# One attention and MLP decode step: the vectors of w2 and wo in blocks of 128 columns, and one spreading of o

## The chip, the cores and the metric

The kernel runs on one core of a Trainium2 chip. Times are device microseconds (us) of one execution. The time before is the median of three runs, 99.37 us (99.36 to 99.45).

A core has five engines with instruction streams of their own: TensorE (PE in the profile, its weight loads PEld) multiplies into PSUM, VectorE (DVE) and ScalarE (ACT) compute elementwise, GpSimd (POOL) fills constants here and counts landings, and SyncE (SP) issues the transfers. Sixteen DMA engines move the data. Engines wait for one another through semaphores.

## The reference

One token x of 1,024 values is normalised to xn. Two branches read xn, and their results are added to x:

```python
x = A_x
xn = _layernorm(x, axis=-1)
return x + _A_ref(xn, A_k_cache, A_v_cache, A_wq, A_wo) + _B_ref(xn, B_w1, B_b1, B_w2, B_b2)
# _A_ref: q = xn @ wq (32 heads of 128); keys and values are the last 4096 of 65536 rows, 4 groups of 8 heads
#         o = softmax(q k^T / sqrt(128)) v ;  o as 4096 values @ wo (4096 x 1024)
# _B_ref: h = gelu(layernorm(xn) @ w1 + b1)  (3584 values);  h @ w2 (3584 x 1024) + b2
```

All inputs are bf16. Almost everything that is moved is weights and cache: wq 8 MB, w1 7, w2 7, wo 8, keys 4 and values 4.

## The kernel before

**Loads.** SP issues, in this order: wq's first half, keys 0, wq's second half, keys 1, w1 (lines 234 to 238); when the keys have been transposed on DVE, the values into the keys' place; when q is done, w2 in parts of 16 and 12 rows into wq's place; and when TensorE's w1 loop is done, wo in parts of 8, 12, 9, 2 and 1 rows (lines 310 to 321). A row is what one matmul contracts over: 128 partitions with 1,024 columns. wo's first 20 rows go to the tile BIG behind w2's 28, the last 12 (TAIL is 20) into the tile KT.

**TensorE in order.** It multiplies xn with wq, then q with the keys, then adds a bias row through EDGE, then multiplies with w1 in a loop of seven (lines 472 to 476), sums the softmax, transposes h, and multiplies the probabilities with the values (lines 488 to 491). Then come twelve rounds (label `pe_round`) that go over 48 rows, four to a round: seven rounds for w2, five for wo's first twenty rows. The twelve rows that are left are an unrolled tail (lines 529 to 540) with four small matmuls to a row. All rounds and the tail add into one PSUM bank.

**Vectors.** In a round the stationary operand is a window of 128 columns of the tile GO, which is zero but for the values wanted. A value stands at two columns 64 apart, so that a window lays it on two output rows; values follow one another two columns apart. GO holds three such vectors, G0 (12 values of h), G1 (16) and OT (32 values of o), of the sizes that PHASES = [3, 4, 5] gives in rounds, and from phase to phase the window jumps by SHIFT more. `twice` is the view that writes both copies. DVE writes G0 and G1 (line 370).

**The o turn.** The attention result ON (32 rows, DVE, line 386) has to become columns. Four matmuls do it at `pe_turn_o` (line 507) into PSUM bank 2, and DVE copies the 32 columns from there, twice each, into OT (line 389). `pe_turn_o` is one block in the loop and is entered at each phase's end but the last, so it is run twice: the first time its result is what DVE copies, the second time it is computed again and the wait asks for DVE's copy instead of ON (register `ready`).

**Counting.** A round waits for the semaphore s_feed to reach the register `turn`. GpSimd counts it up in program order (lines 401 to 414): one for each wq half and for each two transposed key parts, then, as parts of w2 and wo land, their number of rounds, and one for wo's nine rows. `pe_phase` waits for the next count too, so the tail begins when wo's nine rows are counted. GpSimd's constants (lines 177 to 225) stand ahead of that; the memset of GO is their last but one.

Of the kernel before, what the change touches and what calls it, by code (L numbers as in the profile page):

```python
# [5 lines left out]
ALU = mybir.AluOpType  # L6
ACTF = mybir.ActivationFunctionType
AX = mybir.AxisListType

D = 1024  # L10
# [7 lines left out]
FC = F // 128  # L18
# [3 lines left out]
WQ_CHUNKS = [4, 4]  # L22
# [4 lines left out]
PAIRS = 2  # L27
FAR = -1e30
XP = 72
TAIL = 20  # L30
TAIL_AT = [0, 512, 256, 768]
ROW = 31
LEAD = 32
COPY = 64
ROUND = 4
PHASES = [3, 4, 5]
SHIFT = 160


class Track:  # L40
# [11 lines left out]
def bass_parallel_sum__sliding_block_cached__mixer_channel_mlp__decode_kernel(  # L52
# [17 lines left out]
    pe, dve, act, pool, sp = nc.tensor, nc.vector, nc.scalar, nc.gpsimd, nc.sync  # L70

    def sems(name, n):
        return [nc.alloc_semaphore(f"{name}{i}") for i in range(n)]
# [5 lines left out]
    s_wo = sems("s_wo", len(WO_CHUNKS))  # L79
    s_w2 = sems("s_w2", len(W2_CHUNKS))  # L80

    DVE = Track(nc, "S_DVE")
    ACT = Track(nc, "S_ACT")
    POOL = Track(nc, "S_POOL")
    done = {n: nc.alloc_semaphore(f"S_PE_{n}") for n in (
        "x", "h", "hT", "q", "sc", "pv", "tot", "o2", "fin")}
    s_feed = nc.alloc_semaphore("S_FEED")

    def sb(name, shape, d):
        return nc.alloc_sbuf_tensor(name, shape, d)  # L90

    f32, bf16 = dt.float32, dt.bfloat16
# [23 lines left out]
    HT = sb("HT", [128, FC], f32)  # L116
    U2 = sb("U2", [128, FC], f32)
# [9 lines left out]
    SUMP = sb("SUMP", [128, 1], f32)  # L127
    REC = sb("REC", [64, 1], f32)
    ON = sb("ON", [32, DH], bf16)
    starts = [sum(2 * ROUND * n + SHIFT for n in PHASES[:k]) for k in range(3)]  # L130
    GO = sb("GO", [128, starts[2] + 192], bf16)
    G0, G1, OT = (GO[:, first:first + 192 - 8 * (k == 0)] for k, first in enumerate(starts))
    ONM = QBD[0:32, :].bitcast(f32)
    KV = sb("KV", [128, 16384], bf16)
    KT = sb("KT", [128, 16384], bf16)
# [4 lines left out]
    PS = nc.alloc_psum_tensor("PS", [128, 8 * 512], f32)  # L140
# [14 lines left out]
    C = {}  # L155
# [18 lines left out]
    def pool_wait():  # L174
        pool.wait_ge(POOL.sem, POOL.cnt)
# [6 lines left out]
        out=identb[:, :], in_=identb[:, :], pattern=[[-1, 128]], compare_op=ALU.not_equal,  # L182
# [16 lines left out]
        out=identf[:, :], in_=identf[:, :], pattern=[[-1, 128]], compare_op=ALU.not_equal,  # L199
# [15 lines left out]
    POOL.mark(pool.affine_select(  # L215
        out=HALF4[:, :], in_=HALF4[:, :], pattern=[[-16, 4]], compare_op=ALU.is_ge, fill=0.0,
# [26 lines left out]
    def layernorm_stats(src, n, name):  # L243
# [21 lines left out]
        out=XM.rearrange("p (a r) -> p a r", r=KC), in0=XN[:, :].rearrange("p (a r) -> p a r", r=KC),  # L265
        in1=identb[:, :].unsqueeze(2).to_broadcast([128, 128, KC]), op=ALU.mult))
    dve_wait()
    DVE.mark(dve.tensor_reduce(
        out=XNT[:, :], in_=XM.rearrange("p (a r) -> p r a", r=KC), axis=AX.X, op=ALU.add))
# [9 lines left out]
        out=B64[:, :].rearrange("p (k r) -> p k r", k=2),  # L279
        in_=identf[:, :].rearrange("p (q r) -> p r q", q=4).unsqueeze(1).to_broadcast([128, 2, 32, 4]),  # L280
# [36 lines left out]
    c0 = 0  # L317
    for j, n in enumerate(WO_CHUNKS):
        home, first = wo_home(c0)
        sp.dma_start(home[:, first:first + n * D], wo_flat[:, c0 * D:(c0 + n) * D]).then_inc(s_wo[j], 16)  # L320
        c0 += n

    def twice(vec, n):
        return vec[:, LEAD:LEAD + 2 * COPY].rearrange("p (u x) -> p u x", u=2)[:, :, 0:2 * n:2]

    S = PS[:, 3 * 512:7 * 512]
    for n in range(2):
        dve.wait_ge(done["sc"], 14 + 2 * n)
        C["mx"] = DVE.mark(dve.tensor_reduce(  # L329
            out=MX2[:, n:n + 1], in_=S[:, 1024 * n:1024 * n + 1024], axis=AX.X, op=ALU.max))  # L330
# [6 lines left out]
    for b in range(4):  # L337
        C["nmb"] = DVE.mark(dve.tensor_scalar(  # L338
            out=NMB[32 * b:32 * b + 32, :], in0=MXR[:, :], scalar1=-SCALE, scalar2=None, op0=ALU.mult))
    act.wait_ge(DVE.sem, C["nmb"])  # L340
    C["exp"] = ACT.mark(act.activation(  # L341
        out=Pb[:, :], in_=S, func=ACTF.Exp, bias=NMB[:, 0:1], scale=SCALE, accum_out=SUMP[:, 0:1]))
# [9 lines left out]
        out=HT[:, :].rearrange("p (t c) -> p c t", c=4),  # L352
        in0=PS[:, 2 * 512 + 32:2 * 512 + 64].rearrange("p (c t) -> p c t", c=4)[:, :, 0:7],
        in1=B1T[:, :].rearrange("p (t c) -> p c t", c=4), op=ALU.add))
# [11 lines left out]
    dve_wait()  # L366
    DVE.mark(dve.reciprocal(out=U2[:, :], in_=U2[:, :]))
    dve_wait()
    for vec, c0, n in ((G0, 0, PHASES[0] * ROUND), (G1, PHASES[0] * ROUND, PHASES[1] * ROUND)):
        C["d_GT"] = DVE.mark(dve.tensor_tensor(  # L370
            out=twice(vec, n), in0=HT[:, c0:c0 + n].unsqueeze(1).to_broadcast([128, 2, n]),
            in1=U2[:, c0:c0 + n].unsqueeze(1).to_broadcast([128, 2, n]), op=ALU.mult))

    dve.wait_ge(done["tot"], 1)
    DVE.mark(dve.reciprocal(out=REC[:, :], in_=PS[0:64, 2 * 512 + 64:2 * 512 + 65]))
# [2 lines left out]
    for i in range(2):  # L378
        rows = slice(32 * i, 32 * i + 32)
        DVE.mark(dve.scalar_tensor_tensor(  # L380
            out=ONM.rearrange("p (i c d) -> p i c d", i=2, c=PAIRS)[:, i],
            in0=PS[rows, 512:1024].rearrange("p (c i d) -> p i c d", c=PAIRS, i=2)[:, i], scalar=REC[rows, 0:1],
            in1=HALF[rows, :].unsqueeze(2).to_broadcast([32, PAIRS, DH]), op0=ALU.mult, op1=ALU.mult))
    dve_wait()
    with nc.allow_low_precision(reason="one of the four terms is not zero"):
        C["on"] = DVE.mark(dve.tensor_reduce(
            out=ON[:, :], in_=ONM.rearrange("p (g d) -> p d g", g=4), axis=AX.X, op=ALU.add))
    dve.wait_ge(done["o2"], 1)
    C["OT"] = DVE.mark(dve.tensor_copy(
        twice(OT, 32), PS[:, 2 * 512:2 * 512 + 32].unsqueeze(1).to_broadcast([128, 2, 32])))  # L390

    for engine, track, a in ((act, ACT, 1), (dve, DVE, 0)):
        engine.wait_ge(done["fin"], 1)
# [13 lines left out]
    pool.wait_ge(DVE.sem, C["kt", 3])  # L407
    pool.sem_inc(s_feed, 1)
    for semaphores, chunks in ((s_w2, W2_CHUNKS), (s_wo, WO_CHUNKS[:WO_HEAD])):
        for semaphore, n in zip(semaphores, chunks):  # L410
            pool.wait_ge(semaphore, 16)
            pool.sem_inc(s_feed, n // ROUND)
# [15 lines left out]
    turn = pe.alloc_register("turn")  # L428
# [40 lines left out]
    def h_cols(row, t):  # L469
        return row.rearrange("p (m a c) -> p m a c", m=128, a=7)[:, :, bass.ds(t, 1), :]  # L470

    pe.wait_ge(s_w1[0], 16)
    with pe.Fori(0, 7) as t:
        for k in range(KC):
# [15 lines left out]
            last = add(bank(1), PT[:, bass.ds(i * 256 + u * 64, 128)], V3[:, :, bass.ds(i * 1024 + u * 256, 256)])  # L490
        last.then_inc(done["pv"], 1)

    first_turn = 1 + len(WQ_CHUNKS) + PAIRS
    vec, column, limit, more, ready = (pe.alloc_register(n) for n in ("vec", "column", "limit", "more", "ready"))
    for register, value in ((vec, 0), (column, 0), (limit, first_turn + PHASES[0]), (more, PHASES[1]), (ready, C["on"])):
        pe.reg_mov(register, value)
    pe.wait_ge(DVE.sem, C["d_GT"])
    PEO = [pe.engine]
    at = type(pe.snap(turn)).of_register_unchecked
    vec_at, column_at = at(vec, min_val=0, max_val=starts[2] + 2 * ROUND * (PHASES[2] - 1)), at(  # L500
        column, min_val=0, max_val=(sum(PHASES) - 1) * ROUND * D)
    nc.br("pe_round", engines=PEO)
    with nc.body("pe_turn_o", valid_engines=PEO):
        pe.wait_ge(DVE.sem, ready)
        pe.reg_add(ready, ready, C["OT"] - C["on"])
        for j in range(4):
            last = pe.matmul(PS[:, 2 * 512:2 * 512 + 32], lhsT=E4[:, j * 128:(j + 1) * 128],
                             rhs=ON[:, j * 32:(j + 1) * 32], start=(j == 0), stop=(j == 3))
        last.then_inc(done["o2"], 1)
        pe.reg_add(vec, vec, SHIFT)  # L510
        pe.reg_add(limit, limit, more)
        pe.reg_add(more, more, PHASES[2] - PHASES[1])
        nc.br("pe_round", engines=PEO)
    with nc.body("pe_round", valid_engines=PEO):
        pe.wait_ge(s_feed, turn)
        pe.reg_add(turn, turn, 1)
        for u in range(ROUND):
            for a in range(2):
                add(bank(7), GO[:, bass.ds(vec_at + (LEAD + 2 * u - ROW - a), 128)],
                    BIG[:, bass.ds(column_at + (u * D + a * 512), 512)])  # L520
        pe.reg_add(vec, vec, 2 * ROUND)
        pe.reg_add(column, column, ROUND * D)
        pe.br_lt(turn, limit, on_true="pe_round", on_false="pe_phase")
    with nc.body("pe_phase", valid_engines=PEO):
        pe.wait_ge(s_feed, turn)
        pe.br_lt(turn, first_turn + sum(PHASES), on_true="pe_turn_o", on_false="pe_tail")
    nc.switch_bb("pe_tail")

    c0 = TAIL
    for j, n in enumerate(WO_CHUNKS[WO_HEAD:]):  # L530
        pe.wait_ge(s_wo[WO_HEAD + j], 16)
        for c in range(c0, c0 + n):
            home, column = wo_home(c)
            rhs = home[:, column:column + D]
            for a in range(4):
                first, column = LEAD + 2 * c - (0 if a % 2 else ROW), 7 * 512 + a // 2 * 256
                last = add(PS[32 * a:32 * a + 32, column:column + 256], OT[:, first:first + 32],
                           rhs[:, TAIL_AT[a]:TAIL_AT[a] + 256], tile_position=(0, 32 * a))
        c0 += n
# [31 lines left out]
```

## Time and profile before

| what | us |
|---|---|
| median of three runs | 99.37 |
| the profiled execution | 99.39 |
| its span | 98.0 |
| TensorE busy | 73.8 |
| VectorE busy | 38.2 |
| transfers, share of 16 engines, SP's queue | 95.5% |
| w1 loop ends, SP issues wo from | 62.6 |
| rounds begin | 73.13 |
| the tail's first load | 94.33 |
| last landing of wo | 95.89 |
| store issued | 96.79 |

The profile is of one execution. Its lines give, for groups of instructions, the engine, the kernel's line, the operation, and out<-in by the program's names. In the timeline a line starts with start and duration in us, xN is the number of instructions, and brackets hold the engine's idle time ahead of the group and what ended it. In the list of transfers the last number is the us from issue to landing. Because a helper records most matmuls, they all carry line 426 and are told apart by their operands: BIG with XZ is wq, BIG with YZ is w1, BIG with GO the rounds, KT with GO the tail. A few matmul records are missing from the trace.

### The profile page before, as it was taken

What the parts mean: (1) busy time and instruction counts of PE and PEld (TensorE: products, weight loads), DVE (VectorE), ACT (ScalarE), POOL (GpSimd) and SP (SyncE); (2) the same over time, 40 slices, a digit from 0 to 9 for tenths busy, and PEclk for the clock granted to TensorE, in tenths of its full rate; (3) what the DMA queues carried; (4) which work ended last, traced back from release to release, by engine and by line L of the source; (5) the groups of instructions that cost most, each with busy time, mean ns of one, the idle gap of its engine ahead of it and who ended that gap; (6) DMA issues with size and microseconds to landing.
All of it is one profiled execution on the core that took longest, in us unless ns stands there. A gap on an engine that the chain in (4) does not pass through costs nothing.

```text
span 98.0 us, 1273 instructions
## 1 busy us (share of the span) xinstructions
PE 73.8 (75%) x341; PEld 30.9 (32%) x353; DVE 38.2 (39%) x52; ACT 7.8 (8%) x14; POOL 9.3 (9%) x29
## 2 busy tenths in 40 slices
PE   0005000399999974999999999799969999999991
PEld 0001000033444421334434444333334444444450
DVE  0002899899920799950193620060034000000001
ACT  0500000600000023000005200200000000000001
POOL 6999200000000000000000000000000000000000
PEclk9999999999999998557999999999999999999999
DMA  6699999999999988889899999998999999999980
GB/s 201 254 442 429 402 430 442 428 455 428 408 435 528 609 375 375 375 375 468 375 428 428 435 515 455 428 428 375 411 391 428 428 482 421 401 421 451 395 324 1
DMA packets 2229, 39.88 MB, mean 407 GB/s; under 512 B 434, under 2 KB 436, under 8 KB 692
## 3 DMA queue, kind: packets, MB, share of 16 engines
q1 hardware_dynamic: 2020, 39.85, 95.5%
q10 hardware_dynamic: 208, 0.01, 0.1%
q8 instruction: 1, 0.02, 0.1%
HBM read 39.86 MB, written 0.00 MB: 407 GB/s over the span
## 4 chain that ended last, share of the span: by engine, by line
DMA 63%; PE 23%; DVE 8%; SPq 3%; issue 2%
DMA KT<-in_A_wo_dram 32%; DMA KV<-in_A_k_cache_dram 30%; PE PS L426 22%; DVE KT L285 4%; SPq L320 2%; DVE MX L329 1%; SPq L159 1%; DVE QBD L305 1%; DVE Pb L293 1%; SPq L232 1%; DVE Pb L395 0%; PE PS L464 0%
## 5 line engine op out<-in xcount | busy, mean ns | idle before, releaser
L426 PE MATMUL PS<-BIG,GO 128*128 x84 | 20.1, 379 | 1.5 <-DVE QBD L380 0.7
L285 DVE STREAM_TRANSPOSE KT<-KV 128x4096 bf16<-128x4096 bf16 x4 | 17.7, 4432 | 4.9 <-DMA KV<-in_A_k_cache_dram 4.9
L426 PE MATMUL PS<-BIG,XZ 128*128 x64 | 16.5, 426 | 0.0
L426 PEld LDWEIGHTS PS<-BIG,GO 128*128 x96 | 9.2, 98 | 11.6 <-issue 1.2
L426 PE MATMUL PS<-BIG,YZ 128*128 x56 | 12.4, 380 | 0.0
L426 PE MATMUL PS<-KT,QBD 128*128 x32 | 9.9, 486 | 1.6 <-DVE QBD L305 1.6
L426 PEld LDWEIGHTS PS<-BIG,XZ 128*128 x64 | 6.8, 107 | 10.1 <-issue 4.2
L426 PE MATMUL PS<-KV,KT 128*128 x32 | 8.3, 381 | 0.6
L423 PE MATMUL PS<-XBRP,HOT 1*128 1x512 bf16 x3 | 1.7, 618 | 9.0 <-DVE XZ L275 9.0
L426 PEld LDWEIGHTS PS<-BIG,YZ 128*128 x56 | 5.4, 96 | 6.8 <-issue 0.9
L395 DVE CAST Pb<-PS 64x256 bf16<-64x256 f32 x1 | 0.4, 417 | 17.6 <-PE PS L426 17.6
L419 PE MATMUL PS<-XBRP,onesb 1*128 1x512 bf16 x2 | 1.0, 602 | 8.2 <-DMA XBRP<-in_A_x_dram 8.2
L426 PEld LDWEIGHTS PS<-KT,QBD 128*128 x32 | 3.8, 119 | 7.7 <-issue 5.7
L245 DVE BATCH_NORM_STATS2 BN<-PS 128x6 f32<-128x512 f32 x2 | 1.3, 690 | 9.3 <-PE PS L419 9.3
L426 PEld LDWEIGHTS PS<-KV,KT 128*128 x32 | 3.1, 96 | 5.4 <-issue 4.0
L329 DVE TENSOR_REDUCE MX<-PS 128x1 f32<-128x1024 f32 x2 | 2.4, 1220 | 5.5 <-PE PS L426 5.5
L380 DVE SCALAR_TENSOR_TENSOR QBD<-PS,REC,HALF 32x256 f32<-32x256 f32 x2 | 0.9, 474 | 6.9 <-PE PS L426 6.9
L423 PEld LDWEIGHTS PS<-XBRP,HOT 1*128 1x128 bf16 x3 | 0.3, 118 | 10.2 <-DVE XZ L275 9.9
L345 DVE STREAM_TRANSPOSE KT<-Pb 128x2048 bf16<-128x2048 bf16 x1 | 2.3, 2311 | 2.1 <-ACT Pb L341 2.1
L341 ACT ACTIVATE Pb<-PS,NMB 128x2048 bf16<-128x2048 f32 x1 | 2.0, 1967 | 14.1 <-DVE NMB L338 14.1
L395 ACT ACTIVATE Pb<-PS 64x256 bf16<-64x256 f32 x1 | 0.4, 381 | 31.6 <-PE PS L426 31.6
L351 DVE TENSOR_TENSOR HT<-PS,B1T 128x28 f32<-128x28 f32 x1 | 0.2, 206 | 6.6 <-PE PS L482 6.6
(75 smaller groups left out, 36.6 us busy)
## 6 DMA issues: line engine op xcount, KB each, us to landing
BIG<-in_A_wq_dram SPq DMA_DIRECT2D x2, 4096.0 KB, 18.9
BIG<-in_B_w_dram SPq DMA_DIRECT2D x1, 7168.0 KB, 46.2
KV<-in_A_k_cache_dram SPq DMA_DIRECT2D x2, 2048.0 KB, 23.3
KV<-in_A_v_cache_dram SPq DMA_DIRECT2D x2, 2048.0 KB, 13.5
BIG<-in_B_w_dram SPq DMA_DIRECT2D x1, 4096.0 KB, 24.7
BIG<-in_B_w_dram SPq DMA_DIRECT2D x1, 3072.0 KB, 31.4
BIG<-in_A_wo_dram SPq DMA_DIRECT2D x1, 3072.0 KB, 25.5
KT<-in_A_wo_dram SPq DMA_DIRECT2D x1, 2304.0 KB, 30.6
```

The costliest lines, as they stand in the source:

```text
L159: sp.dma_start(dst[:, c0 * width:(c0 + n) * width].rearrange("p (c n) -> p c n", c=n), src[:, c0:c0 + n, :],).then_inc(semaphores[j], 16)
L232: sp.dma_start(KV[:, c * 8192:(c + 1) * 8192], pairs(A_k_cache, c)).then_inc(s_k[c], 16)
L245: DVE.mark(dve.bn_stats(out=BN[:, 12 * n + 6 * i:12 * n + 6 * i + 6], in_=src[:, 512 * i:512 * i + 512]))
L285: C["kt", n] = DVE.mark(dve.transpose(KT[:, n * 4096:(n + 1) * 4096], KV[:, n * 4096:(n + 1) * 4096]))
L293: C["qtb"] = DVE.mark(dve.transpose(QTB, Q32))
L320: sp.dma_start(home[:, first:first + n * D], wo_flat[:, c0 * D:(c0 + n) * D]).then_inc(s_wo[j], 16)
L329: C["mx"] = DVE.mark(dve.tensor_reduce(out=MX2[:, n:n + 1], in_=S[:, 1024 * n:1024 * n + 1024], axis=AX.X, op=ALU.max))
L341: C["exp"] = ACT.mark(act.activation(out=Pb[:, :], in_=S, func=ACTF.Exp, bias=NMB[:, 0:1], scale=SCALE, accum_out=SUMP[:, 0:1]))
L345: C["d_pt"] = DVE.mark(dve.transpose(PT[:, 0:2048], Pb[:, :]))
L419: last = pe.matmul(bank(i), lhsT=onesb[0:1, :], rhs=XB[0:1, 8 * i:8 * i + 8, :])
L423: pe.matmul(bank(n), lhsT=HOT[:, 8:136], rhs=XB[0:1, 0:8, :], start=True, stop=False, skip_group_check=True)
L426: return pe.matmul(to, lhsT=lhsT, rhs=rhs, start=False, stop=False, skip_group_check=True, **place)
```

## The change

GO is laid out by rounds. It now holds twelve blocks of 128 columns (STEP), one for each round, w2's seven first and then wo's five, and behind them OT with the twelve values of o for the tail only. In a block the four values stand two columns apart and once more 64 columns on. The window moves by STEP from round to round, without jumps.

DVE writes all seven blocks of w2 in one instruction. The o turn is run once, after four rounds (TURN), and then the limit of the loop is set to all twelve. ScalarE, not DVE, copies from PSUM: first the 20 columns that the rounds use, into the five blocks, then the 12 of the tail, without a second copy. TensorE's rounds no longer wait for that copy themselves; GpSimd waits for it ahead of its first count for wo. Three of the five register moves of the loop go ahead of w1's loop, and two are gone.

```diff
-PHASES = [3, 4, 5]
-SHIFT = 160
+ROUNDS = 12
+TURN = 4
+STEP = 128
...
-    GO = sb("GO", [128, starts[2] + 192], bf16)
-    G0, G1, OT = (GO[:, first:first + 192 - 8 * (k == 0)] for k, first in enumerate(starts))
+    GO = sb("GO", [128, ROUNDS * STEP + LEAD + 96], bf16)
+    OT = GO[:, ROUNDS * STEP + LEAD:]
...
-    def twice(vec, n):
-        return vec[:, LEAD:LEAD + 2 * COPY].rearrange("p (u x) -> p u x", u=2)[:, :, 0:2 * n:2]
+    def spread(first, n):
+        return GO[:, LEAD + first * STEP:LEAD + (first + n) * STEP].rearrange(
+            "p (r c y) -> p r c y", c=2, y=COPY)[:, :, :, 0:2 * ROUND:2]
+
+    def rows_of(values):
+        n = values.shape[1] // ROUND
+        return values.rearrange("p (r u) -> p r u", u=ROUND).unsqueeze(2).to_broadcast([128, n, 2, ROUND])
...
-    for vec, c0, n in ((G0, 0, PHASES[0] * ROUND), (G1, PHASES[0] * ROUND, PHASES[1] * ROUND)):
-        C["d_GT"] = DVE.mark(dve.tensor_tensor(
-            out=twice(vec, n), in0=HT[:, c0:c0 + n].unsqueeze(1).to_broadcast([128, 2, n]),
-            in1=U2[:, c0:c0 + n].unsqueeze(1).to_broadcast([128, 2, n]), op=ALU.mult))
+    C["d_GT"] = DVE.mark(dve.tensor_tensor(
+        out=spread(0, FC // ROUND), in0=rows_of(HT[:, :]), in1=rows_of(U2[:, :]), op=ALU.mult))
...
-    dve.wait_ge(done["o2"], 1)
-    C["OT"] = DVE.mark(dve.tensor_copy(
-        twice(OT, 32), PS[:, 2 * 512:2 * 512 + 32].unsqueeze(1).to_broadcast([128, 2, 32])))
+    act.wait_ge(done["o2"], 1)
+    o2 = PS[:, 2 * 512:2 * 512 + 32]
+    ACT.mark(act.activation(out=spread(FC // ROUND, TAIL // ROUND), in_=rows_of(o2[:, 0:TAIL]), func=ACTF.Copy))
+    C["OT"] = ACT.mark(act.activation(
+        out=OT[:, LEAD:LEAD + 2 * (32 - TAIL):2], in_=o2[:, TAIL:32], func=ACTF.Copy))
...
     for semaphores, chunks in ((s_w2, W2_CHUNKS), (s_wo, WO_CHUNKS[:WO_HEAD])):
+        if semaphores is s_wo:
+            pool.wait_ge(ACT.sem, C["OT"])
         for semaphore, n in zip(semaphores, chunks):
...
+    first_turn = 1 + len(WQ_CHUNKS) + PAIRS
+    vec, column, limit = (pe.alloc_register(n) for n in ("vec", "column", "limit"))
+    PEO = [pe.engine]
+    for register, value in ((vec, 0), (column, 0), (limit, first_turn + TURN)):
+        pe.reg_mov(register, value)
     pe.wait_ge(s_w1[0], 16)
...
-    first_turn = 1 + len(WQ_CHUNKS) + PAIRS
-    vec, column, limit, more, ready = (pe.alloc_register(n) for n in ("vec", "column", "limit", "more", "ready"))
-    for register, value in ((vec, 0), (column, 0), (limit, first_turn + PHASES[0]), (more, PHASES[1]), (ready, C["on"])):
-        pe.reg_mov(register, value)
     pe.wait_ge(DVE.sem, C["d_GT"])
...
     with nc.body("pe_turn_o", valid_engines=PEO):
-        pe.wait_ge(DVE.sem, ready)
-        pe.reg_add(ready, ready, C["OT"] - C["on"])
+        pe.wait_ge(DVE.sem, C["on"])
...
-        pe.reg_add(vec, vec, SHIFT)
-        pe.reg_add(limit, limit, more)
-        pe.reg_add(more, more, PHASES[2] - PHASES[1])
+        pe.reg_mov(limit, first_turn + ROUNDS)
         nc.br("pe_round", engines=PEO)
...
-        pe.reg_add(vec, vec, 2 * ROUND)
+        pe.reg_add(vec, vec, STEP)
...
-                first, column = LEAD + 2 * c - (0 if a % 2 else ROW), 7 * 512 + a // 2 * 256
+                first, column = LEAD + 2 * (c - TAIL) - (0 if a % 2 else ROW), 7 * 512 + a // 2 * 256
```

More of the change, by code (lines that the diff above doesn't have):

```diff
@@ L129, in bass_parallel_sum__sliding_block_cached__mixer_channel_mlp__decode_kernel @@
     ON = sb("ON", [32, DH], bf16)
-    starts = [sum(2 * ROUND * n + SHIFT for n in PHASES[:k]) for k in range(3)]
-    GO = sb("GO", [128, starts[2] + 192], bf16)
-    G0, G1, OT = (GO[:, first:first + 192 - 8 * (k == 0)] for k, first in enumerate(starts))
+    GO = sb("GO", [128, ROUNDS * STEP + LEAD + 96], bf16)
+    OT = GO[:, ROUNDS * STEP + LEAD:]
     ONM = QBD[0:32, :].bitcast(f32)
@@ L491, in bass_parallel_sum__sliding_block_cached__mixer_channel_mlp__decode_kernel @@
         last.then_inc(done["pv"], 1)
-    first_turn = 1 + len(WQ_CHUNKS) + PAIRS
-    vec, column, limit, more, ready = (pe.alloc_register(n) for n in ("vec", "column", "limit", "more", "ready"))
-    for register, value in ((vec, 0), (column, 0), (limit, first_turn + PHASES[0]), (more, PHASES[1]), (ready, C["on"])):
-        pe.reg_mov(register, value)
     pe.wait_ge(DVE.sem, C["d_GT"])
-    PEO = [pe.engine]
     at = type(pe.snap(turn)).of_register_unchecked
-    vec_at, column_at = at(vec, min_val=0, max_val=starts[2] + 2 * ROUND * (PHASES[2] - 1)), at(
-        column, min_val=0, max_val=(sum(PHASES) - 1) * ROUND * D)
+    vec_at, column_at = at(vec, min_val=0, max_val=STEP * (ROUNDS - 1)), at(
+        column, min_val=0, max_val=(ROUNDS - 1) * ROUND * D)
     nc.br("pe_round", engines=PEO)
     with nc.body("pe_turn_o", valid_engines=PEO):
-        pe.wait_ge(DVE.sem, ready)
-        pe.reg_add(ready, ready, C["OT"] - C["on"])
+        pe.wait_ge(DVE.sem, C["on"])
         for j in range(4):
@@ L525, in bass_parallel_sum__sliding_block_cached__mixer_channel_mlp__decode_kernel @@
         pe.wait_ge(s_feed, turn)
-        pe.br_lt(turn, first_turn + sum(PHASES), on_true="pe_turn_o", on_false="pe_tail")
+        pe.br_lt(turn, first_turn + ROUNDS, on_true="pe_turn_o", on_false="pe_tail")
     nc.switch_bb("pe_tail")
```

## The prediction

> **What bounds the kernel now.** I read the page first. TensorE is busy for three quarters of the span and no other engine for half of it, while the row of the DMA engines stands at nines from the second slice nearly to the end: the queue that SP fills takes 95.5% of what sixteen engines have.
>
> ```profile
> span 98.0 us, 1273 instructions
> ...
> PE 73.8 (75%) x341; PEld 30.9 (32%) x353; DVE 38.2 (39%) x52; ACT 7.8 (8%) x14; POOL 9.3 (9%) x29
> ...
> DMA  6699999999999988889899999998999999999980
> ...
> q1 hardware_dynamic: 2020, 39.85, 95.5%
> ```
>
> The stream has no slack inside either. One line, 9 ns plus the bytes at 27.2 bytes per ns, fits its packets' medians at every size and in every tile: 0.084 us for 2,048 bytes, 0.611 for 16,384, 1.213 for 32,768, 2.116 for 57,344. So an engine does nothing between packets, from about 2 us until its last packet, 95.45 us on the last engine.
>
> Then the chain of waits, for what ends last: the last issue of wo (64.38) lands 31.52 us later, at 95.89. Behind it come four small matmuls, a copy and the store.
>
> ```profile
> 64.38 31.52 DMA KT<-in_A_wo_dram
> 95.89 0.04 issue
> 95.94 0.32 PE PS L426 x4
> 96.26 0.02 issue
> 96.28 0.42 DVE Pb L395
> ```
>
> Then the timeline of TensorE in the stage that the change edits, and the landings of wo:
>
> ```profile
> 73.13 5.13 PE L426 MATMUL PS<-BIG,GO 128*128 x21 [0.74 <-DVE QBD L380]
> ...
> 78.19 0.26 PE L507 MATMUL PS<-ON,E 32*128 32x32 bf16 x4
> ...
> 78.61 6.85 PE L426 MATMUL PS<-BIG,GO 128*128 x28 [0.16 <-issue]
> ...
> 85.40 0.26 PE L507 MATMUL PS<-ON,E 32*128 32x32 bf16 x4
> ...
> 85.82 8.58 PE L426 MATMUL PS<-BIG,GO 128*128 x35 [0.16 <-issue]
> 94.33 1.10 PEld L426 LDWEIGHTS PS<-KT,GO 128*32 128x32 bf16 x44 [0.42 <-DMA KT<-in_A_wo_dram]
> 94.33 1.39 PE L426 MATMUL PS<-KT,GO 128*32 128x256 bf16 x44
> 95.94 0.10 PEld L426 LDWEIGHTS PS<-KT,GO 128*32 128x32 bf16 x4 [0.51 <-DMA KT<-in_A_wo_dram]
> ```
>
> ```profile
> BIG<-in_A_wo_dram SPq DMA_DIRECT2D x1, 3072.0 KB, 25.5
> KT<-in_A_wo_dram SPq DMA_DIRECT2D x1, 2304.0 KB, 30.6
> ```
>
> The rounds look like a full engine right up to the tail, and that is the trap. The nine rows of wo were issued at 63.43 and land 30.6 later, at 93.99. GpSimd's count for them is recorded at 94.01, TensorE's branch into the tail, which waits for that count, at 94.06, the first weight load of the tail at 94.33. So a landing opens the tail, and a later landing (95.89) opens its last row. TensorE sits idle for about 0.2 us before that row.
>
> **The change, part by part.** The sum is made against the profiled execution: 99.39 us, of which 98.0 are span and 1.39 lie around it. The median of the runs is 99.37, so 0.02 goes off at the end.
>
> 1. Vectors. GO grows from 568 to 1,664 columns, and its memset with it. From 569 ns at 568 columns (L222) and 995 ns at 1,088 (L185) a column costs 0.82 ns, so 569 + 1,096 x 0.82 = 1.47 us, 0.90 more. GpSimd's constants then end at about 11.4 instead of 10.5. Their readers are DVE at 18.41 (L278) and TensorE at 19.57 (first load of wq); those 7 us of cover hide it, and without them it would delay the q chain by 0.9. GpSimd's own next step, the count for wq's first half, waits for a landing at 13.0 (issue 0.81, 12.2 to landing) anyway. The tiles after GO move up; the packet line above holds for tiles at all their offsets, so I price another address at nothing (bounds: plus and minus the 1 to 2 ns by which sizes miss the line, under 0.2% of a packet).
>
> 2. DVE writes the 28 columns of w2 in one instruction for two (189 and 194 ns, overlapping by 0.09). 56 elements: 0.21 by the slope of the two, at most 0.38. DVE then waits for the attention sum until 72.4 anyway; cover 6.9 us (the wait before L380), cost 0.
>
> 3. Register moves. Five moves stand between the attention matmuls and the first round, 0.088 apart in the trace (72.07 to 72.46). Three of them now stand before the w1 loop. There the sequencer resumes when the second EDGE load is released (49.79), and the first w1 load follows at 50.11; three moves put 0.26 in front of it. They delay w1's end, and with it SP's issue of wo (62.59), to about 62.85; the queue then still holds w2, which lands at 76.3, so wo loses nothing with 13 us of cover. Behind the attention 0.44 goes away. Rounds start 0.18 earlier: cost minus 0.18 on TensorE, 0 at the end.
>
> 4. The o turn. After the last matmul of a phase (77.88) the next would start 0.216 later, at 78.10; it starts at 78.61. A turn costs 0.515 and there were two (78.10 to 78.61, 85.30 to 85.82). One stays, after the fourth round: minus 0.515 on TensorE. It still waits for ON, ready at 74.6, and comes at about 79.9. The branch before it asks for the count of w2's second part, which GpSimd gave at 76.31: 3 us of cover.
>
> 5. ScalarE's copies. With rounds from 72.95 and 0.216 a matmul, the 32 matmuls of four rounds end near 79.9; the DVE cast started 0.61 after the last round matmul, so ScalarE starts near 80.3. The trace has no such copy. Nearest rows: 225 ns (L363, 28 columns), 233 (the cast of the same data on DVE), 587 (L347, 512 columns from PSUM). Two: 0.4 to 1.2, taken as 0.45, since their columns are near 28. Copies after the exponential needed no table load (L347). OT stands at about 80.75, at worst 81.5. ScalarE has nothing queued behind but the final copy at 96.28.
>
> 6. GpSimd's wait for OT. Behind it on GpSimd stand the counts for all of wo. The first has 81.18 as its landing, so OT is normally there first. At worst the count comes at 81.5, and round 8 asks for it near 85.2. Cost 0 with 3.7 us of cover.
>
> 7. What is late next. TensorE has gained 0.18 + 0.515 = 0.695. Round 10 would start at 89.27 - 0.695 = 88.57, and its sequencer asks some 0.3 earlier, at 88.2. But wo's twelve rows, issued at 62.96, land 25.5 later, at 88.49 (GpSimd's count at 88.51). From such a request to the first matmul took 0.355 at 72.78, so round 10 starts near 88.87 and the last round matmul near 88.87 + 23 x 0.216 = 93.84, against 94.02. Of 0.695 about 0.5 is eaten here. The rest is lost at the branch, which still waits for 94.01.
>
> Sum at the end: 0. The last landing, 95.89, is SP's stream; 99.39 + 0, less 0.02: 99.37.
>
> [...]
>
> **The rivals.**
>
> Faster: in executions without the profiler the rounds, not the landings, could open the tail. For it speaks that TensorE's last round matmul (94.02 plus 0.216) ends only 0.1 before the tail's first load. All of the 0.695 would then show: 98.68. Against it: the last row waits 0.2 for its landing even so, and unprofiled times (99.36 to 99.45) surround the profiled 99.39. So TensorE would have to be later than in the trace by more than that before the first tenth could show. Chance 0.09.
>
> Slower, by an instruction packet. One packet of the program comes late:
>
> ```profile
> q8 instruction: 1, 0.02, 5.7%
> ```
>
> This is the DMA view of 95.45 to 96.5. The packet has 16,384 bytes, starts at 95.46, 10 ns after the stream's last packet, and takes 0.96. If it came ahead of the last row's packets on its engine, the last landing would be 0.96 later: 100.33. That decides once the request moves up past the packets then queued, eight of 0.085: between 0 and 0.7 us. What sends for it is most likely TensorE in the unrolled tail. [...] Chance 0.06. [...]
>
> Slower, by the new wait: OT more than 3.7 us later than reckoned holds all counts of wo, and each us beyond that, less the slack of 0.2, is paid in full: at 5 us late, 100.5. A slow copy or a table load (1.28 us on L252) does not reach that. Chance 0.03. For transfers slowed after all by the new addresses, 0.05 more: half a percent on each packet of a stream of 93 us is 0.47, so 99.84.
>
> That nothing changes is the forecast: 0.77.
>
> **How the numbers follow.** 0.2% is 0.20 us, about what a measurement of this kernel can tell from no change. No change, 0.77, has its own range of 99.30 to 99.47 (the runs' spread and half as much again). Faster 0.09; slower 0.06 + 0.03 + 0.05 = 0.14. The range takes in the no-change case whole, to about 0.2 on either side, and the nearest parts of the others: 99.20 to 99.60.
>
> **What would show it.** Right: L507 with four matmuls; the memset of GO at 1.47 us; two ScalarE copies near 80.3; a gap on TensorE before round 10 near 88.5; the first tail load still at 94.3; the last landing at 95.9. Wrong: a tail that opens earlier together with a shorter time (the landings did not bound it), q8's packet before the last 2,048-byte packets, or a first wo count on GpSimd after 85.

## The result and the profile after

The changed kernel takes 99.25 us (median; 99.1 to 99.5) beside 99.38 for the kernel before on the same chip. The ratio is 0.9984, with a 95% interval of 0.9977 to 0.9991: faster by 0.16%, where no change was forecast. It is a small step, yet more than the runs leave to chance. It is also the difference of two larger ones, neither of which the prediction had: the transfers end 0.42 us earlier, and 0.24 us more passes outside the profiled span.

The first can be read at once. The profiled execution takes 99.20 us, of which 97.55 are span; before, 99.39 and 97.98. So the span is 0.42 shorter, but what lies around it has grown from 1.41 to 1.65. First the page of the changed kernel, its span, engines and queue:

```profile
span 97.6 us, 1259 instructions
...
PE 71.6 (73%) x337; PEld 30.1 (31%) x349; DVE 37.9 (39%) x50; ACT 8.1 (8%) x16; POOL 10.2 (10%) x29
...
DMA  7599999999999998888999999999899998999980
...
q1 hardware_dynamic: 2020, 39.85, 95.7%
```

The same 2,020 packets and 39.85 MB are still the bound: their share of the engines' time stands at 95.7% against 95.5%. DVE has 50 instructions for 52, ACT 16 for 14. Next the chain of waits, in order of time, start and duration:

```profile
49.68 12.46 PE PS L433 x56
...
63.95 31.52 DMA KT<-in_A_wo_dram
95.48 0.04 issue
95.52 0.32 PE PS L433 x4
95.84 0.02 issue
95.87 0.42 DVE Pb L400
```

From the last issue of wo on it has the links of before, 0.42 earlier: the last row of wo is issued at 63.95 (64.38 before) and takes 31.52, as before. That the two durations are equal is chance, for different things held the issues. Here the w1 loop (the 56 matmuls at 49.68) began when w1 had landed, at 49.33. In the profile of before w1 landed at 49.48, but the loop waited longer, for the work on q, whose matmuls ran with the granted clock (the share of its full clock that TensorE is given) at half from 38.4 to 45.2 us:

```profile
49.80 0.39 PE PS L464
50.18 12.39 PE PS L426 x56
```

E2 and E3 below have addresses like the old ones and a w1 loop opened by w1's landing. There the last row takes 31.86 and 31.81, so part of the gain is made on wo itself. In the list of transfers w1 has this (46.2 before):

```profile
BIG<-in_B_w_dram SPq DMA_DIRECT2D x1, 7168.0 KB, 46.0
```

Now TensorE and ScalarE in the stage that was edited:

```profile
72.24 6.85 PE L433 MATMUL PS<-BIG,GO 128*128 x28 [0.28 <-issue]
79.03 0.26 PE L513 MATMUL PS<-ON,E 32*128 32x32 bf16 x4
79.33 0.22 ACT L393 ACTIVATE GO<-PS 128x40 bf16<-128x40 f32 x1 [15.07 <-PE PS L513]
79.43 0.18 ACT L394 ACTIVATE GO<-PS 128x12 bf16<-128x12 f32 x1
79.45 8.58 PE L433 MATMUL PS<-BIG,GO 128*128 x35 [0.16 <-issue]
88.56 5.13 PE L433 MATMUL PS<-BIG,GO 128*128 x21 [0.53 <-POOLq L419]
93.81 1.48 PE L433 MATMUL PS<-KT,GO 128*32 128x256 bf16 x44
95.52 0.29 PE L433 MATMUL PS<-KT,GO 128*32 128x256 bf16 x4 [0.22 <-DMA KT<-in_A_wo_dram]
```

One o turn is left, and the two ScalarE copies stand behind it. At 88.56 there is a new wait of 0.53 us, for GpSimd's count (line 419) of wo's second part. The last row waits 0.22 for its landing, as the 0.2 before. All of this is what the prediction drew, 0.3 to 1.0 us earlier.

Where the stream gained shows when its landings are laid beside one another. The lead of the changed kernel grows from load to load (from the landing records, us):

| last landing of | before | after | lead |
|---|---|---|---|
| keys 1 | 27.639 | 27.554 | 0.085 |
| w1 | 49.479 | 49.326 | 0.153 |
| values | 59.271 | 59.040 | 0.231 |
| w2, second part | 76.285 | 76.014 | 0.271 |
| wo, first part | 81.180 | 80.865 | 0.315 |
| wo, nine rows | 93.986 | 93.606 | 0.380 |
| wo, last row | 95.895 | 95.477 | 0.418 |

From w1's landing to the last row of wo 46.416 us pass before and 46.151 after. In this stretch the gain is no event but a rate, and the packet records show it. The same sizes take less, and have stopped varying (mean, with the lowest and highest in brackets, ns):

| packet, bytes | before | after |
|---|---|---|
| 24,576 | 915.7 (912 to 921) | 912.0 (912 to 912) |
| 18,432 | 690.1 (686 to 696) | 686.0 (686 to 686) |
| 16,384 | 613.3 | 611.1 |
| 4,096 | 161.9 | 159.0 |
| 2,048 | 85.5 | 84.0 |
| 57,344 | 2,116.9 | 2,116.0 |

The longer packets of before stand almost all behind w1. The 16,384-byte packets of keys 1 take 611.2 ns in the mean (611.0 after); those of the values, which go to the same tile later, take 613.6 and 614.5. Against the durations of after, the packets of before hold 0.02 us per engine from 13 to 48 us, and 0.24 from there on. These 0.24 are nearly all of the 0.265 that the stream gains behind w1. The lead of 0.153 at w1's landing does not stand in the packets' durations. It is also within what executions differ by: in the profiles of the runs below that share the new addresses, w1 lands between 49.22 and 49.84.

### The profile page after: what moved, and what is told of

Same layout as the page of the kernel before. It is cut to its first block, busy times and chain, and to the rows that moved or that the text cites. A ratio compares the mean times of both kernels' runs of the same rounds, so it can differ in the third digit from the quotient of the medians.

```text
span 97.6 us, 1259 instructions
## 1 busy us (share of the span) xinstructions
PE 71.6 (73%) x337; PEld 30.1 (31%) x349; DVE 37.9 (39%) x50; ACT 8.1 (8%) x16; POOL 10.2 (10%) x29
## 3 DMA queue, kind: packets, MB, share of 16 engines
q1 hardware_dynamic: 2020, 39.85, 95.7%
## 4 chain that ended last, share of the span: by engine, by line
DMA 79%; PE 13%; SPq 4%; issue 1%; DVE 0%
DMA BIG<-in_B_w_dram 47%; DMA KT<-in_A_wo_dram 32%; PE PS L433 13%; SPq L320 2%; SPq L232 1%; SPq L159 1%; DVE Pb L400 0%
## 5 line engine op out<-in xcount | busy, mean ns | idle before, releaser
L433 PE MATMUL PS<-KT,QBD 128*128 x32 | 8.0, 379 | 2.6 <-DVE QBD L305 1.8
L433 PEld LDWEIGHTS PS<-KT,QBD 128*128 x32 | 3.1, 96 | 7.5 <-issue 5.4
```

The source lines that it names most:

```text
L433: return pe.matmul(to, lhsT=lhsT, rhs=rhs, start=False, stop=False, skip_group_check=True, **place)
```

## The experiments

GO is 2,192 bytes longer on each partition, so the tiles behind it, which take all the large transfers, moved. In the built programs they moved by 2,176: they began 128 bytes past a multiple of 256 and now begin on one. All kernels below compute the full result.

**Theory:** this move sets the packets' durations, and TensorE's 0.7 us is worth nothing. **Rival:** the shorter path of TensorE, or ScalarE's copies, made the gain, and the packets only go with it.

**E1: the kernel before, at the new addresses.**

```diff
-    GO = sb("GO", [128, starts[2] + 192], bf16)
+    GO = sb("GO", [128, 1664], bf16)[:, 0:starts[2] + 192]
```

> The kernel before, with nothing changed but the space that GO takes: 3,328 bytes as after, so that KV, KT and BIG stand where they stand after (their start is 256 past a multiple of 512, before it was 128). Address theory (the transfers' packets are some 4 ns shorter at the new addresses, which adds up over the stream): packets of 24,576 bytes all at 912 ns instead of 912 to 920, last landing near 95.5 in the profile, time ratio to before 0.9984, about 99.2 us. TensorE theory (the shorter TensorE chain gave the time): no change, 99.38 us, ratio 1.000, and packets as before. Chance theory (the packets differ from execution to execution, not with the address): packets as they fall, ratio 1.000.

Measured: 99.0 us, ratio 0.9956 (0.9942 to 0.9971). The mean of the 24,576-byte packets is 912.1 ns and wo's last row lands at 95.480. Its chain of waits:

```profile
63.95 31.53 DMA KT<-in_A_wo_dram
95.48 0.04 issue
95.52 0.32 PE PS L426 x4
```

These are the changed kernel's numbers to 0.01, without any of its logic. So the addresses alone shorten the span by 0.42. E1 is also 0.25 faster than the changed kernel, where the address theory expected the two to be equal: something in the new logic costs.

**E2: the changed kernel, moved off again** by 64 unused columns behind GO.

```diff
-    GO = sb("GO", [128, ROUNDS * STEP + LEAD + 96], bf16)
+    GO = sb("GO", [128, ROUNDS * STEP + LEAD + 96 + 64], bf16)[:, 0:ROUNDS * STEP + LEAD + 96]
```

> The changed kernel with 128 bytes of unused space behind GO, so that KV, KT and BIG start 384 past a multiple of 512, that is 128 past a multiple of 256 as before. Address theory with 256 bytes as the step that counts: packets spread over 912 to 920 ns again and the gain is gone, 99.38 us, ratio 1.000. TensorE theory: the gain stays, 99.2 us, ratio 0.9984, whatever the packets do.

Measured: 99.77 us, 1.0037 (1.0024 to 1.0049); packets of 24,576 bytes 915.7 ns again. The chain:

```profile
64.17 31.86 DMA KT<-in_A_wo_dram
...
96.06 0.32 PE PS L433 x4
...
96.41 0.42 DVE Pb L400
```

The new logic at addresses like the old ones is slower than the kernel before by 0.37%, where 1.000 was expected, although TensorE has less to do. Both directions give 0.4 to 0.5 us for the addresses.

**E3 and E4: which multiple.** E3 moves the kernel before by 32 bytes (GO of 592 columns), E4 the changed kernel by 256 bytes, onto a multiple of 512.

```diff
+    GO = sb("GO", [128, 592], bf16)[:, 0:starts[2] + 192]                                              # E3
+    GO = sb("GO", [128, ROUNDS * STEP + LEAD + 96 + 128], bf16)[:, 0:ROUNDS * STEP + LEAD + 96]   # E4
```

> The kernel before with 32 bytes more behind GO, so that KV, KT and BIG start 160 past a multiple of 512, no longer at a multiple of 64. Address theory: packets at least as long as before (916 ns or more for 24,576 bytes), time 99.38 us or up to 0.3 more, ratio 1.000 to 1.003. TensorE theory and chance theory: ratio 1.000.

> The changed kernel with 256 bytes of unused space behind GO, so that KV, KT and BIG start at a multiple of 512. Address theory: packets as short as after (912 ns for 24,576 bytes) or shorter, time 99.1 to 99.25 us, ratio 0.997 to 0.9985. TensorE theory: as after, 0.9984. It tells the theories apart only where it comes out under 0.997 or near 1.000; its use is the size of the step, 256 or 512.

Measured: E3 99.47 us, 1.0003 (0.9994 to 1.0012), 915.7 ns; E4 99.19, 0.9973 (0.9964 to 0.9983), 912.0 ns. 160 bytes past a multiple costs what 128 past does, and 512 gives nothing that 256 did not. Over all the profiles the rate separates the addresses without overlap: from w1's landing to the last row of wo the three kernels off a multiple of 256 (before, E2, E3) take 46.42 to 46.46 us, and sixteen of the seventeen on one 46.12 to 46.17. The seventeenth is E18.

**E5: the copies back on DVE**, all else as in the changed kernel; GpSimd then waits for DVE.

```diff
-    act.wait_ge(done["o2"], 1)
+    dve.wait_ge(done["o2"], 1)
...
-    ACT.mark(act.activation(out=spread(FC // ROUND, TAIL // ROUND), in_=rows_of(o2[:, 0:TAIL]), func=ACTF.Copy))
+    DVE.mark(dve.tensor_copy(spread(FC // ROUND, TAIL // ROUND), rows_of(o2[:, 0:TAIL])))
...
```

> The changed kernel, but DVE instead of ScalarE copies o's columns from PSUM, and GpSimd waits for DVE's copy. The first four runs leave a puzzle: at the same addresses the changed kernel takes 99.25 us and the kernel before 99.0, and of the profiled executions' time 1.65 us lie outside the span with the new logic and 1.41 with the old. ScalarE theory (moving the copies to ScalarE costs it, by two more instructions there and two fewer on DVE): 99.0 us, 1.41 outside the span, ratio 0.9957. Any other part of the logic: 99.25 us, 1.65 outside, ratio 0.998.

Measured: 99.03 us, 0.9952 (0.9935 to 0.997), the same as E1's 99.0. What costs is that the copies left DVE, though in the changed kernel they end at 79.61 and GpSimd, which waits for them next, has no count to give before 80.865, when wo's first part lands. In the profile of E5 the end of the span is not earlier but later than in the changed kernel:

```profile
64.15 31.51 DMA KT<-in_A_wo_dram
95.66 0.04 issue
95.70 0.32 PE PS L432 x4
```

The gain lies outside the span: 1.42 us around it for 1.65. E5 against E1 is also the test of TensorE's 0.7 us: at the same addresses and with the copies on the same engine, new and old logic take 99.03 and 99.0 us, which is less apart than the intervals of either can tell.

**E6 and E8: the other parts, added to E1.** E6 makes GpSimd wait for OT ahead of wo's counts; E8 lets the memset of GO run over all 1,664 columns.

```diff
+        if semaphores is s_wo:                        # E6
+            pool.wait_ge(DVE.sem, C["OT"])
...
-    POOL.mark(pool.memset(GO[:, :], 0.0))             # E8
+    POOL.mark(pool.memset(GOALL[:, :], 0.0))
```

> The kernel before at the addresses of after (as the first run), and GpSimd waits for DVE's copy of o ahead of its first count for wo, as it waits for ScalarE's after. Wait theory (GpSimd's wait costs 0.25): 99.25 us, ratio 0.998, 1.65 outside the span. Otherwise: 99.0 us, ratio 0.9957, 1.41 outside; the copy is done 2.5 us ahead of wo's first landing, so the count cannot be later.

> The kernel before at the addresses of after, with the memset over all 1,664 columns of GO's space, as after. Every theory: the memset takes 1.47 us, the constants end near 11.4 us, nobody waits for them, 99.0 us, ratio 0.9957. If it comes to 99.25, the longer memset is what costs.

Measured: 98.95 and 98.93 us, 0.9948 (0.9929 to 0.9968) and 0.9948 (0.9927 to 0.9968). Neither shows a cost.

**E7, E9, E10, E12, E11: whose program length counts.** The change also alters how many instructions each engine's compiled program has. DVE has 74 for 76: the joined write of w2's vectors saves one, the copy that went to ScalarE the other. ScalarE has 40 for 38, TensorE 305 for 308. (The profiles record fewer, 56 for 58 on DVE and 22 for 20 on ScalarE, with the same differences.) An added wait is not always an instruction of its own: three come out as two, 28 as 14. E7 gives the changed kernel three more on TensorE by waits for landings long past. E9 and E12 give E1 two more and one more on ScalarE, as waits; E10 two as copies into an unused tile. E11 gives E1 one more on DVE, by moving the copy of H8 there from ScalarE.

```diff
+    for landed in (s_x, s_wq[0], s_wq[1], s_k[0], s_k[1]):     # E7, TensorE, changed kernel
+        pe.wait_ge(landed, 16)
...
+    for early, count in (("x", 1), ("q", 8), ("sc", 16)):      # E9; E12 without the first
+        act.wait_ge(done[early], count)
...
+    for first, end in ((0, 40), (40, 52)):                     # E10
+        ACT.mark(act.activation(out=SCRATCH[:, first:end], in_=identf[:, first:end], func=ACTF.Copy))
...
-    C["a_h8"] = ACT.mark(act.activation(out=H8, in_=bank(0, 8), func=ACTF.Copy))
+    C["a_h8"] = DVE.mark(dve.tensor_copy(H8, bank(0, 8)))      # E11
```

> The changed kernel with five waits more on TensorE, all long satisfied, ahead of the bias row (48 us), so that TensorE's program has 308 instructions as before instead of 305, and its tail begins at the same place. Program theory (the length or the place of TensorE's program sets the time outside the span): 99.0 us, 1.41 outside, ratio 0.9957. Otherwise 99.25 us, 1.65 outside, ratio 0.998. The waits themselves take at most 0.4 us of TensorE at 48 us, less than its gain.

> The kernel before at the addresses of after, with waits on semaphores that are long satisfied added on ScalarE, so that its program has 40 instructions as after instead of 38; no copy is added or moved. Length theory (ScalarE's longer program costs the 0.25 outside the span): 99.25 us, ratio 0.998, 1.65 outside. Work theory (two activations more, whatever the program's length): 99.0 us, ratio 0.9957, 1.41 outside. DVE theory (two instructions fewer on DVE cost it): 99.0.

> The kernel before at the addresses of after, with two idle copies on ScalarE of 128x40 and 128x12 from a constant tile into an unused one behind all others; ScalarE's program has 40 instructions as after. Length theory and work theory: 99.25 us, ratio 0.998, 1.65 outside. DVE theory (two instructions fewer there): 99.0 us, 1.41 outside.

> As the run with two added instructions on ScalarE, but with one: 39 instructions. Length theory by the instruction: 99.12 us, 1.53 outside the span. A step: either 99.0 and 1.41 or 99.25 and 1.65. Work theory and DVE theory: 99.0 us, 1.41 outside.

> The kernel before at the addresses of after, with the copy of h (8x512) on DVE instead of ScalarE: ScalarE's program has 37 instructions. Length theory by the instruction (0.12 each): 98.9 us, ratio 0.9945, about 1.29 outside the span. Length theory with a step between 38 and 40, work theory and DVE theory: 99.0 us, ratio 0.9957, 1.41 outside.

Measured: E7 99.25 us, 0.9978 (0.9967 to 0.9989), still 1.61 to 1.70 around the span. E9 99.0, E10 98.93, E12 98.95 (0.9952, 0.9954 and 0.9948, each within 0.993 to 0.997), all with 1.35 to 1.45 around it. E11 99.14, 0.9973 (0.9962 to 0.9983), with 1.45 to 1.69. So the lengths of TensorE's and ScalarE's programs don't matter. VectorE's is left, and E11 points to it.

**E13 to E18: VectorE's program made longer**, with waits for landings long past. E13 and E16 bring the changed kernel back to 76 instructions, late and early in the program; E17 to 75. E14, E15 and E18 bring E1 to 78, 80 and 90.

```diff
+    for landed in (s_x, s_b2, s_b1):        # E13 (changed kernel), E14 (E1); E17: s_x alone;
+        dve.wait_ge(landed, 16)             # E15: seven landings; E18: 28 such waits
     for engine, track, a in ((act, ACT, 1), (dve, DVE, 0)):
...
+    dve.wait_ge(POOL.sem, C["ones"])        # E16, ahead of the statistics of x; a third wait stands further on
+    dve.wait_ge(s_x, 16)
```

> The changed kernel (copies on ScalarE) with waits that are long satisfied added on DVE ahead of its last copy, so that DVE's program has as many instructions as before (two more than the changed kernel's). DVE-length theory (the length of DVE's program sets what lies outside the span; the changed kernel is two short of a length that costs 1.41): 99.0 us, ratio 0.9955, 1.41 outside. Who-copies theory (it is a DVE that did no copy out of PSUM late in the program that costs it, whatever the length): 99.25 us, ratio 0.998, 1.65 outside.

> The changed kernel with two instructions more on DVE early in its program (satisfied waits at 9 and 18 us) and none late. DVE-length theory: 99.0 us, 1.41 outside, as with the late ones. If only the late ones mend it, the place counts and not the length. Who-copies theory: 99.25 us, 1.65.

> The kernel before at the addresses of after, with two instructions more on DVE, long satisfied waits ahead of its last copy; ScalarE is as before. DVE-length theory with a period of four instructions: two past a good length is as bad as two short, 99.25 us, 1.65 outside. DVE-length theory as a threshold (too short costs): 99.0 us, 1.41. Who-copies theory: 99.0 us, 1.41.

> As the run before it, with four instructions more on DVE than the kernel before. Period of four: good again, 99.0 us, ratio 0.9955, 1.41 outside. Threshold and who-copies theory: 99.0 us, 1.41 too. A cost that grows with each instruction from the kernel before: over 99.25, 1.65 or more.

> The changed kernel with one satisfied wait on VectorE before its last copy, so that VectorE's program has 75 instructions for 74. Theory that the time around the span goes by where VectorE's program meets a fetch of 8,192 bytes of instructions (recorded 1.54 us after the span's end at 77 and 78 instructions, at the span's end at 80, not at 74 and 76): no rule for 75 follows, but the span stays at 97.5 to 97.75 and the time around it lies between the 1.65 of 74 and the 1.41 of 76, so 98.95 to 99.25. Rival, that any change of the program gives a chance value: below 1.35 or above 1.7.

> The kernel before at the moved addresses with 14 more instructions on VectorE before its last copy, 90 for 76. Theory of the fetch: the 8,192 bytes are asked for earlier still, well inside the span, as 80 instructions had them at its end, so the time around the span stays at about 1.2 or less and the whole at 98.7 to 98.95; the fetch is in the trace before 97. Rival, that the time around the span repeats with the program's length or scatters by chance: 1.4 or more, 99.0 or more, with no such packet inside the span.

Measured, with the time that the runs spend outside their spans, and when, after the span's start, the profile's records have a packet of 8,192 bytes of queue 14, which carries instructions. Spans are on record to 0.1 us, so each value outside is good to 0.05.

| VectorE's instructions | kernels | time, us | ratio (95%) | outside the span, us | 8,192-byte packet at |
|---|---|---|---|---|---|
| 74 | changed kernel, E2, E4, E7 | 99.25 (changed) | 0.9984 | 1.60 to 1.78 | none recorded |
| 75 | E17 | 98.77 | 0.9944 (0.9927, 0.9962) | 1.22 to 1.27 | none recorded |
| 76 | before, E1, E3, E5, E6, E8, E9, E10, E12 | 99.0 (E1) | 0.9956 | 1.35 to 1.46 (before mostly 1.40) | none recorded |
| 76 | E13 | 99.16 | 0.9972 (0.9962, 0.9983) | 1.35 to 1.46 | none recorded |
| 76 | E16 | 99.18 | 0.9967 (0.9955, 0.9979) | 1.37 to 1.41 | none recorded |
| 77 | E11 | 99.14 | 0.9973 (0.9962, 0.9983) | 1.45 to 1.69 | 99.09 |
| 78 | E14 | 99.21 | 0.9977 (0.9965, 0.9989) | 1.38 to 1.62 | 99.08 |
| 80 | E15 | 98.92 | 0.9958 (0.9944, 0.9971) | 1.22 to 1.25 | 97.51 |
| 90 | E18 | 99.56 | 1.0019 (1.0009, 1.0028) | 1.21 to 1.29 | 82.12 |

The time outside the span goes with the number of VectorE's instructions. It is 1.60 to 1.78 in all four kernels of 74 and 1.35 to 1.46 in all eleven of 76, with old logic or new, at old addresses or new. Whether the added ones stand early or late (E16, E13) makes no difference to it. The other lengths have one kernel each, and they follow no smooth function: 75 gives 1.25 between 1.65 at 74 and 1.41 at 76, which neither my count of instructions nor an expected value between the two allows. E17's rival, that any change of the program gives a chance value, had named a time below 1.35. The kernels that agree at 74 and at 76 speak against it, but for a single length nothing does. E11, E14 and E15, with about 1.57, 1.51 and 1.25, did not come out at a value that was expected either.

The fetch of 8,192 bytes moves as a longer program would have it: from 1.3 to 1.4 us behind the span's end (77 and 78; not the 1.54 of E17's expectation) to 0.1 us ahead of it (80) and 16 us ahead (90). For 80 and 90 the time around the span stands at its lowest, as the theory of the fetch has it. At 74 to 76, where no such packet is recorded after the span's start, it explains nothing. So it is shown that the time outside the span goes with VectorE's length where a length was tried in several kernels; by what means is open.

E13 and E16 have the expected 1.41 around the span, but their medians, 99.16 and 99.18, stay above the expected 99.0. Two things are seen in their profiles. First, the added waits are not free where they stand late. In E13 the last of them is done behind the wait for the last matmul, and DVE's last copy starts 0.10 us after ScalarE's:

```profile
95.96 0.38 ACT L402 ACTIVATE Pb<-PS 64x256 bf16<-64x256 f32 x1 [16.26 <-PE PS L435]
96.06 0.42 DVE L402 CAST Pb<-PS 64x256 bf16<-64x256 f32 x1 [21.84 <-PE PS L435]
```

In E14, E15 and E18 it is 0.10 too, in E17 0.07; in E1 and E16, which have no late waits, the two start together. Second, the last row lands at 95.568 (E13) and 95.686 (E16), for 95.477 in the changed kernel. This delay is all there when w1 lands (49.418 and 49.528 for 49.326), so it comes from the start of the stream and from no slower rate behind it. The single runs of E16 lie in two groups, 98.87 to 98.91 and 99.17 to 99.21: executions of one kernel differ in this way, and why is open.

E14's profile shows one thing more. The clock stood at half from 38.6 to 45.4 us, and with the old logic the tail is then opened by the rounds, at 94.41, and not by a landing (the nine rows had landed at 93.658). ScalarE's last copy starts 0.43 us after the last landing there and 0.39 after it in E1. In such an execution TensorE's shorter path would be worth 0.04 us.

E18's forecast of at most 98.95 us missed, and its profile shows why: the fetch falls into the stream there. The DMA view of its profile from 82.0 to 82.6 us has

```profile
q14 instruction: 1, 0.01, 3.2%
```

and the packet of 24,576 bytes behind it takes 1,449 ns for 912. It ends at 83.874; begun at the fetch's start (82.119), it would have ended 0.84 earlier. wo's second part, which landed at 88.191 in E1, lands at 88.860, and the last row at 96.144 for 95.480, as its chain shows:

```profile
63.83 32.31 DMA KT<-in_A_wo_dram
96.14 0.04 issue
96.19 0.32 PE PS L428 x4
```

Its last row was issued 0.12 earlier than E1's and still lands 0.66 later. Until the fetch its stream was 0.15 ahead (wo's first part lands at 80.716 for 80.862), so the stream lost 0.81. E15, which has the same time around its span and no such packet in the stream, is 0.64 faster.

**The best of them.** E17, the changed kernel with a single satisfied wait on VectorE, takes 98.77 us (five runs), by the ratios 0.4% under the changed kernel; E1's family, the old logic at the new addresses, lies at 98.93 to 99.0. Both beat both kernels.

## Why the prediction was wrong, and where it was right

- **Step 1, vectors: wrong.** The memset was right (1.48 us measured for 1.47; GpSimd's constants end at 11.4). The failed sentence is "I price another address at nothing", with its bounds of 1 to 2 ns a packet. It measured -0.41 us (E1) to -0.5 (E2). The claim behind it, one line that fits the medians of every size to 1 or 2 ns, did not hold in the trace of before: the line gives 912.5 ns at 24,576 bytes and 686.6 at 18,432, where the medians are 916 and 691. Every tile in question stood off the 256-byte grid, so their agreement with one another said nothing of a tile that is on it. The rival with slower transfers had the right mechanism with the wrong sign. What the runs show in place of the step: behind w1 the stream takes 0.24 to 0.34 us less on the grid than off it, and 0.24 of that stands in the packets' durations. That the rest, gained ahead of w1, comes of the addresses too is shown by the times of E1 and E2 alone; by what means is open.
- **The sum's frame: wrong.** The working set 1.39 us around the span and carried it over. It became 1.65, 0.24 against the kernel, when steps 2 and 5 took one instruction each off VectorE; with two put back (E5, E13, E16) it is 1.41 again. The prediction gave both steps a price at their place on the path, which was right, and none for the program's length, which was the larger.
- **The number: luck.** That 99.25 comes as near to the forecast 99.37 as it does is because these two errors, -0.42 and +0.24, largely cancel.
- **Steps 2 and 3: right on the path.** The one vector instruction takes 0.225 us (0.21 predicted). The three moves stand at 48.61 to 48.78, ahead of w1's landing at 49.33, so they delay nothing at all where 0.26 behind a cover was written.
- **Steps 4 and 5: right.** One turn with four matmuls; the copies take 0.22 and 0.18 (0.45 together was taken) and start at 79.33 for "near 80.3", mostly because rounds began at 72.24 for 72.95. They began 0.89 earlier than before. Of this 0.46 lies between the end of the w1 loop and the rounds, where the register moves were; 0.43 is the earlier w1 loop. In this execution TensorE's mean granted clock was 1.0, in that of before 0.965, with the work on q at half. Such differences of the clock (0.965 to 1.0 in the runs of before) appear among executions of one kernel and go with no difference in time that these runs show.
- **Step 6: right.** E6 puts a price of 0 on the wait (98.95 for 99.0).
- **Step 7: right, and well sized.** The count for wo's second part comes at 88.15, the request at 88.205, and the first matmul follows 0.355 later, at 88.56: the mechanism and the 0.355 of the prediction. The tail is still opened by a landing (93.606, first load 93.805), and E5 against E1 (99.03 and 99.0) shows no gain from TensorE's 0.695 us.
- **The rivals.** Rounds that open the tail: not in the changed kernel, as step 7 says, but E14 shows that with the old logic they can. An instruction packet ahead of the stream's last ones: it did come 0.53 earlier, at 94.928, which was listed as a sign that the prediction is wrong, but it starts as the first engine writes its last packet (94.922), so most likely on an engine that had ended its part (the records do not name it), and the last row landed early all the same. In the profiles of before and after it starts 1.13 and 1.12 us behind the tail's first load, which fits TensorE as its sender but does not show it. That such a packet can cost nearly what the rival says is shown by E18 (0.81 us for 0.96). The new wait: no.

## What to carry to other kernels

Where the transfers are the bound, check first what the change does to the addresses of the tiles that they fill, and look at the spread of the packets of one size, not only at their median: packets that vary by a few ns at constant size (24,576 bytes: 912 to 921 ns) could be made quicker here (912). An edit's sign is not the sign of its idea: undo the layout and the logic separately (E1, E2) before a gain or a loss is put down to either. When two kernels differ by some tenths of a us, split the time into the span and what lies outside, since here one or two instructions more or less on VectorE, far from the critical path too (E16), moved the second by 0.2 to 0.4 us.

## What the runs showed of the hardware

- Packets into tiles that begin on a multiple of 256 bytes take 912 ns at 24,576 bytes and 686 at 18,432, in the changed kernel without spread, in other runs but for a few long ones; into tiles 128 or 160 past one they take 915.7 and 690.0 to 690.4 in the mean. The offset is not all: in the same tile off the grid the packets of keys 1 take 611.2 ns, those of the values 613.6 and 614.5, for 611.0 on the grid. What else it needs is open. Only the tiles that the packets write were moved, so the runs say nothing of the side that is read. E3's 160 shows no difference to the 128 of before (915.7 ns in both).
- The time outside the profiled span goes from 1.21 to 1.78 us with VectorE's program length between 74 and 90 instructions, not monotonically, and does not follow ScalarE's length (37 to 40) or TensorE's (305 to 308).
- A fetch of 8,192 bytes of instructions in the midst of a full stream cost the stream 0.81 us (E18 against E1), though the packet itself is recorded with 0.31.
